# Two thirds of a feed-forward layer's first product by Winograd's seven block products instead of eight

## The chip, the cores and the metric

The kernel runs on one core of one Trainium2 chip. The metric is device time of one execution, in microseconds; a lower time is better. Times of unprofiled runs are given as a median. A profiled execution has its own time, and its span runs from its first to its last instruction. The engines are PE (matrix products; PEld is its loading of weights), DVE (vector), ACT (scalar functions), POOL, and SP, which issues the transfers.

## What is computed

A block-local attention feeds a two-layer feed-forward. Cut to what matters:

```python
# q, k, v: (8, 8, 576, 64); chunks of 64 positions, no attention across chunks
scores = scale * np.matmul(q_c, k_c.transpose(0, 1, 2, 4, 3))
attn = np.exp(scores - max); attn = attn / (sum + 1e-09)
x = np.matmul(attn, v_c)              # put together to (4608 tokens, 512)
h = x @ w_in                          # w_in  (512, 2048)
g = h - np.tanh(h)
out = (g @ w_out).astype(np.float32)  # w_out (2048, 512)
```

The two products of the feed-forward are nearly all of the arithmetic. Each float32 operand is kept as a high and a low part, and a product is three passes: high by high, low by high and high by low.

## The kernel before

The 4608 tokens are nine groups of 512. A group has four tiles of 128 tokens; the program also calls a tile a pair, since it holds two chunks of attention. For one group, `gemm1` makes 128 of the 2048 hidden columns (one `fc` of 16) for all 512 tokens: 3 passes by 4 slices `kc` of the contraction, 12 products with a moving operand of 512 columns, in one PSUM bank `ph`. `shrink` reads that bank: ACT makes the tanh, DVE subtracts, ACT and DVE make the two parts of `g` (`gh`, `gl`). `gemm2` takes the 128 hidden columns of `g` as weights, 12 products of 512 columns, into the four banks `po`. `FeedForward.run` lets `gemm2` follow `gemm1` by two `fc`s, so PE always has two `fc`s of `g` in hand.

Groups 0 and 1 have their parts in the type float32r. From group 2 on (`self.half`, L401) both layers use float16 parts. The weights are turned into float16 by `Half.convert`, three vector and scalar instructions for each `fc`: the 16 of the first layer and 3 of the second in group 1, the other 13 of the second layer in group 2. A converted tile is written over the float32 tile of the `fc` before.

The attention of group g+1 is worked while PE does the feed-forward of group g. The class `Late` has its steps, and `interleaved` puts them at half-steps of `run`: for each tile `split` (the values in two parts), `scores` (L157), `softmax` (L293 to L301), `transpose` (L307, L308 and a transposing transfer, L310) and `values` (L321), whose result goes into the parts `xh`, `xl` of the next group (L324, L325). `BASE` and `STEPS` say at which half-step; `values` is set ten half-steps after `split` and eight after `scores`. The order on each engine is set by a planner from priorities and its own costs. Only the beginning of the program has an order written out by hand (`PLAN`).

On each engine the instructions run in the order of the program. DVE and ACT carry both the `shrink` of the running group and the attention of the next; an instruction that waits holds up all behind it on that engine. SP issues loads, transposing transfers and stores in one order as well.

Of the kernel before, what the change touches and what calls it, by code (L numbers as in the profile page):

```python
# [11 lines left out]
F32 = mybir.dt.float32  # L12
F32R = mybir.dt.float32r
# [9 lines left out]
P = 128  # L23
# [16 lines left out]
WS = 2  # L40
AHEAD = 3
EARLY_FC = 8
# [15 lines left out]
def attn_ffn_kernel(ctx: ExitStack, tc: tile.TileContext, qkE, vE, qL, kL, vL, w_in, w_out, out):  # L58
# [38 lines left out]

    def new_half_x():

        t = xpool.tile([P, KC, MOST], F32R, name="xh").bitcast(F16)  # L100
        return t[:, :, :MOST], t[:, :, MOST:]

    def power(pool, name, sums, to, back):
# [10 lines left out]
        nc.vector.reciprocal(out=to, in_=back)  # L114

    def largest(a, out):

        nc.vector.tensor_reduce(out=out, in_=a, axis=AX.X, op=ALU.max, apply_absolute_value=True)
        nc.vector.tensor_scalar_mul(out, out, 2.0 ** -12)

# [119 lines left out]
    class Late:  # L240
# [4 lines left out]
        def __init__(self, pool):  # L245
            self.pool, self.st = pool, defaultdict(dict)

            self.raw = {n: xpool.tile([P, KC, MOST], F32R, name="xl").bitcast(F32) if n == "q" else pool.tile([P, MOST // P, H * CH], F32, name=f"raw{n}", bufs=1) for n in "qkv"}
            self.v16, self.a, self.aT = [], [], []
            self.room([pool.tile([P, 2, DM], F16, name=f"v16{a}", bufs=1).rearrange("p a n -> p (a n)") for a in "hl"])  # L250

        def two_banks(self):

            return ps_a.tile([P, 2, 4 * P], F32, name="psa")

# [5 lines left out]

        def load(self, p, i):
            for n, src in (("q", qL), ("k", kL), ("v", vL)):
                nc.sync.dma_start(out=self.raw[n][:, i], in_=src[p - NE])

        def powers(self, g):

            d = self.st[f"g{g}"]
            top, to, back = (self.pool.tile([P, 1], F32, name=n, bufs=2) for n in ("sums", "to", "from"))
            largest(self.raw["v"][:, :SIZES[g]].rearrange("p i n -> p (i n)"), top)  # L270
            power(self.pool, "x", top, to, back)
            d["to"] = to_x[g] = to
            from_x[g] = back

        def split(self, g, p, i):
            to = self.st[f"g{g}"]["to"]
            v = self.raw["v"][:, i].rearrange("p (a d) -> p a d", d=D)
# [6 lines left out]
        def scores(self, p, i):  # L284
            q, k = (self.raw[n][:, i].rearrange("p (hp c t) -> p hp c t", hp=4, c=2) for n in "qk")
            self.st[p]["ps"] = quarters(self.two_banks(), lambda r, hp, c: q[r, hp, c, :], lambda r, hp, c: k[r, hp, c, :], "u")

# [24 lines left out]

        def values(self, p, x, i):
            d = self.st.pop(p)
            xh, xl = x
            ps = self.two_banks()[:, 0].rearrange("p (hp c k) -> p hp c k", hp=4, c=2)
            for hp in range(4):
                for c in range(2):
                    cs = slice(c * CH, (c + 1) * CH)
                    for k, (a, b) in enumerate(((0, 0), (0, 1), (1, 0))):  # L320
                        nc.tensor.matmul(ps[:, hp, c, :], lhsT=self.v16[p % len(self.v16)][a][:, c, hp, :], rhs=d["a16"][:, b, hp, cs], start=(k == 0), stop=(k == 2))  # L321
            ts = slice(i * P, (i + 1) * P)
            ps = ps.rearrange("p hp c k -> p hp (c k)")
            nc.scalar.mul(xh[:, :, ts], ps, 2.0 ** -14)  # L324
            nc.vector.scalar_tensor_tensor(out=xl[:, :, ts], in0=ps, scalar=2.0 ** -14, in1=xh[:, :, ts], op0=ALU.mult, op1=ALU.subtract)  # L325

    def interleaved(att, g, x):

        at = defaultdict(list)
        base, first = (LATER, 5) if g == 2 else (BASE, 0)  # L330
        if g == 2:
            for i in range(SIZES[g]):
                at[0].append(lambda i=i: att.load(FIRST[g] + i, i))
        at[first + 2].append(lambda: att.powers(g))
        for i in range(SIZES[g]):
            p = FIRST[g] + i
            fs = [lambda p=p, i=i: att.split(g, p, i), lambda p=p, i=i: att.scores(p, i), lambda p=p: att.softmax(p),
                  lambda p=p: att.transpose(p), lambda p=p, i=i: att.values(p, x, i)]
            for k, f in zip(STEPS, fs):
                at[base[i] + k].append(f)  # L340
            if g + 1 < NG and i < SIZES[g + 1]:
                at[base[i] + STEPS[1] + 1].append(lambda i=i: att.load(FIRST[g + 1] + i, i))
        return at

    class Half:
# [4 lines left out]
        def __init__(self, pool):  # L350
            self.pool = pool
            self.to_h = const.tile([P, 1], F32, name="to_h")
            self.to, self.back = (const.tile([P, 2], F32, name=n) for n in ("to_w", "from_w"))

        def powers(self):
# [19 lines left out]
        def convert(self, part, fc, place):  # L375
# [6 lines left out]
            nc.vector.scalar_tensor_tensor(out=l16, in0=l, scalar=to, in1=l16, op0=ALU.mult, op1=ALU.add)  # L382

        def power_of(self, g):
            sig, to, undo = (const.tile([P, 1], F32, name=n, bufs=2) for n in ("sig", "to_g", "undo_g"))
            nc.vector.tensor_mul(sig, from_x[g], self.back[:, 0:1])
            nc.vector.scalar_tensor_tensor(out=to, in0=to_x[g], scalar=4.0, in1=self.to_h, op0=ALU.mult, op1=ALU.mult)
            nc.vector.tensor_scalar(out=to, in0=to, scalar1=2.0 ** 100, scalar2=TINY, op0=ALU.min, op1=ALU.max)
            nc.vector.reciprocal(out=undo, in_=to)
            nc.vector.tensor_mul(undo, undo, self.back[:, 1:2])  # L390
            return sig, to, undo


    class FeedForward:
# [3 lines left out]
        def __init__(self, g, x):  # L398
            self.g, self.x, self.queue, self.po = g, x, [], []
# [8 lines left out]
        def room(self, pool, tiles):  # L408
            self.po += [pool.tile([P, DM], F32, name=f"po{t}") for t in tiles]

# [53 lines left out]

        def finish(self):
            assert not self.queue
            for t in range(SIZES[self.g]):
                ot = outs[t] if outs else ffn.tile([P, DM], F32, name="t", bufs=3)
# [9 lines left out]
                r = (FIRST[self.g] + t) * P  # L478
                nc.sync.dma_start(out=out[r:r + P, :], in_=ot)


# [83 lines left out]
    att, half = Late(late), Half(late)  # L565
    for g in range(1, NG):
        x, nx = nx, new_half_x() if g + 1 < NG else None
        ff = FeedForward(g, x)
        ff.room(ps_o1, range(2))
        ff.room(ps_o2, range(2, SIZES[g]))  # L570
        at = interleaved(att, g + 1, nx) if nx else {}
        if g == 1:
            half.powers()
            first_place = late.tile([P, DM], F32, name="first_place", bufs=1).bitcast(F16)
            for fc in range(FC):

                at[2 * fc + 1].append(lambda fc=fc: half.convert(0, fc, place_of("l", 0, fc - 1) if fc else first_place))

            def more(k):

                t = [place_of("h", 0, fc) for fc in (range(6) if k == 0 else range(6, 12))]
                if k == 0:
                    att.room(t[0:2])
                    att.a += [a.rearrange("p (a n) -> p a n", a=2) for a in t[2:4]]
                else:
                    att.aT += [a.rearrange("p (i q) -> p i q", i=8) for a in t[0:2]]
                    outs.extend(a.bitcast(F32) for a in t[2:6])

            at[12].append(lambda: more(0))
            at[2 * FC + 2].append(lambda: more(1))  # L590

        for fc in range(FC):
            if g == (1 if fc < AHEAD else 2):
                k = 2 * FC + 2 * (LAG - AHEAD + fc) - 3 if g == 1 else 2 * (fc - AHEAD) + 1
                at[k].append(lambda fc=fc: half.convert(1, fc, place_of("l", 1, fc - 1) if fc else place_of("h", 0, 13)))
        ff.run([(fc, 0, SIZES[g]) for fc in range(FC)], at)

# [40 lines left out]
```

## Time and profile before

| | us |
|---|---|
| median of 3 runs (849.85 to 850.09) | 849.96 |
| the profiled execution | 849.57 |
| its span | 847.8 |
| PE busy | 829.4 (98%) |
| DVE busy | 536.2 (63%) |
| ACT busy | 396.7 (47%) |
| granted TensorE clock, mean | 0.992 |

The page has the share of the span that each engine was busy. A busy share is a mean over stages with different limits, so the stages are looked at apart: group 1 runs from about 140 to 228.5 us, group 2 from 228.5 to 316.8, and from there on every group takes 89 us. [...] Idle time of an engine that is not the bound costs nothing.

### The profile page before, as it was taken

The numbers are of one execution on the slowest core, as the hardware profiler recorded it, in microseconds if no ns is written. First come the engines' busy times: TensorE is split into PE (matmuls) and PEld (weight loads), VectorE is DVE, ScalarE is ACT, GpSimd is POOL, SyncE is SP. The second block draws the span as 40 slices with busy tenths as digits, with TensorE's granted clock in tenths as the row PEclk, the third lists the DMA queues.
The fourth block names the chain that finished last, engine by engine and source line by source line (L and its number), as shares of the span: only waits on it lengthen the run. The fifth ranks groups of instructions, "written<-read, shape, count | busy, mean of one in ns | idle before, by whom it ended". The sixth has DMA issues, their size and how long they took to land.

```text
span 847.8 us, 13865 instructions
## 1 busy us (share of the span) xinstructions
PE 829.4 (98%) x5645; PEld 458.1 (54%) x5645; DVE 536.2 (63%) x922; ACT 396.7 (47%) x729; POOL 8.7 (1%) x19
## 2 busy tenths in 40 slices
PE   5899999999999999999999999999999999999997
PEld 2687788778744444444444444444444444444443
DVE  5997897878997755565556555564567446633232
ACT  5898874445664443334343443434344334423222
POOL 0000001000000000000000000000000000000000
PEclk7899999999999999999999999999999999999999
DMA  9735234222212212221221121321222100110001
GB/s 358 278 110 200 100 101 149 63 52 74 75 51 68 58 44 81 51 74 27 88 63 50 51 86 39 76 50 63 63 55 59 50 14 13 20 56 1 1 1 50
DMA packets 53823, 62.76 MB, mean 74 GB/s; under 512 B 32256, under 2 KB 32256, under 8 KB 53760
## 3 DMA queue, kind: packets, MB, share of 16 engines
q1 hardware_dynamic: 53760, 61.88, 23.6%
q8 instruction: 44, 0.72, 0.3%
q14 instruction: 19, 0.16, 0.1%
HBM read 45.09 MB, written 9.44 MB: 64 GB/s over the span
## 4 chain that ended last, share of the span: by engine, by line
PE 87%; DVE 7%; ACT 3%; issue 1%; DMA 1%; SPq 0%; DVEq 0%; ACTq 0%
PE po L447 41%; PE ph L418 40%; PE psa L321 2%; PE psa L157 2%; DVE w L137 1%; DVE w L136 1%; DVE wl L382 1%; DVE wl L381 1%; ACT w L134 1%; ACT s L201 1%; ACT wh L141 1%; DMA raw<-w_out 1%; DVE wl L142 1%; DVE w L135 0%; PE ps L157 0%
## 5 line engine op out<-in xcount | busy, mean ns | idle before, releaser
L418 PE MATMUL ph<-xh,wl 128*128 128x512 f16 (+2 forms) x1404 | 324.3, 378 | 0.1
L447 PE MATMUL po<-wl,gh 128*128 128x512 f16 (+1 forms) x968 | 300.4, 381 | 0.0
L418 PEld LDWEIGHTS <-wl 128*128 128x128 f16 x1260 | 120.1, 98 | 140.7 <-issue 0.4
L447 PE MATMUL po<-wl,gl 128*128 128x512 f16 x420 | 159.2, 379 | 0.0
L434 DVE SCALAR_TENSOR_TENSOR gl<-t,to_g,gh 128x512 f16<-128x512 f32 x112 | 84.1, 751 | 108.4 <-ACT gh L433 108.4
L427 DVE SCALAR_TENSOR_TENSOR t<-ph,sig,t 128x512 f32<-128x512 f32 x112 | 83.8, 748 | 98.4 <-ACT t L426 97.8
L447 PEld LDWEIGHTS <-gh 128*128 128x128 f16 x896 | 87.3, 98 | 104.3
L433 ACT ACTIVATE gh<-t,to_g 128x512 f16<-128x512 f32 x112 | 80.8, 721 | 130.9 <-PE po L447 104.7
L426 ACT ACTIVATE t<-ph,sig 128x512 f32<-128x512 f32 x112 | 76.8, 685 | 117.6 <-PE ph L418 116.7
L447 PEld LDWEIGHTS <-gl 128*128 128x128 f16 x448 | 43.8, 98 | 52.8
L447 PE MATMUL po<-wh,gh 128*128 128x512 f32 (+1 forms) x184 | 67.7, 393 | 1.6 <-ACT gh L438 1.6
L447 PE MATMUL po<-wh,gl 128*128 128x512 f32 (+1 forms) x156 | 61.0, 393 | 0.2 <-DVE gl L439 0.2
L295 ACT ACTIVATE s<-s 128x512 f32<-128x512 f32 x28 | 17.6, 630 | 59.6 <-DVE s L294 59.4
L418 PE MATMUL ph<-xh,wh 128*128 128x512 f32 (+1 forms) x144 | 37.5, 377 | 1.7 <-ACT xh L237 1.2
L307 ACT CAST wh<-s 128x512 f16<-128x512 f32 x27 | 16.7, 618 | 45.9 <-DVE s L301 45.8
L418 PE MATMUL ph<-xl,wh 128*128 128x512 f32 (+1 forms) x144 | 35.6, 368 | 0.0
L380 ACT ACTIVATE wl<-wh,to_w 128x512 f16<-128x512 f32 x30 | 21.6, 722 | 24.0 <-DVE wl L382 12.7
L297 DVE TENSOR_REDUCE sm<-s 128x8 f32<-128x512 f32 x28 | 19.2, 685 | 18.2 <-ACT s L295 18.2
L418 PEld LDWEIGHTS ph<-xh,wh 128*128 128x128 f32 x144 | 24.9, 188 | 7.7 <-ACT wh L141 1.7
L308 DVE TENSOR_TENSOR wh<-s,wh 128x512 f16<-128x512 f32 x27 | 18.7, 692 | 15.9 <-ACT wh L307 15.7
L438 ACT CAST gh<-t 128x512 fp32r<-128x512 f32 (+1 forms) x36 | 20.5, 570 | 16.6 <-PE po L447 14.3
L447 PEld LDWEIGHTS po<-wh,gh 128*128 128x128 f32 x128 | 24.0, 188 | 7.5 <-ACT gh L438 2.5
(114 smaller groups left out, 840.8 us busy)
## 6 DMA issues: line engine op xcount, KB each, us to landing
raw<-w_in SPq DMA_DIRECT2D x16, 512.0 KB, 4.0
raw<-w_out SPq DMA_DIRECT2D x16, 512.0 KB, 5.0
out<-wh SPq DMA_DIRECT2D x32, 256.0 KB, 2.4
rawk<-kL SPq DMA_DIRECT2D x28, 256.0 KB, 3.0
rawv<-vL SPq DMA_DIRECT2D x28, 256.0 KB, 2.6
xl<-qL SPq DMA_DIRECT2D x28, 256.0 KB, 2.8
qk<-qkE SPq DMA_DIRECT2D x8, 512.0 KB, 5.7
v<-vE SPq DMA_DIRECT2D x8, 256.0 KB, 5.6
```

The source lines that it names most:

```text
L157: nc.tensor.matmul(ps[os, r, hp * CH:(hp + 1) * CH], lhsT=lhsT(rs, hp, o), rhs=rhs(rs, hp, o), start=True, stop=True)
L295: nc.scalar.activation(s, s, AF.Exp, scale=scale)
L297: nc.vector.reduce_sum(out=sm[:, :, 0], in_=s, axis=AX.X)
L308: nc.vector.tensor_sub(a[:, 1], sf, a[:, 0])
L380: nc.scalar.activation(h16, h, AF.Copy, scale=to)
L418: nc.tensor.matmul(ph, lhsT=self.weight(fc, 0, a)[:, kc * P:(kc + 1) * P], rhs=x[b][:, kc, cols], start=(k == 0), stop=(k == 3 * KC - 1))
L426: nc.scalar.activation(t, ph, AF.Tanh, scale=self.sig)
L427: nc.vector.scalar_tensor_tensor(out=t, in0=ph, scalar=self.sig, in1=t, op0=ALU.mult, op1=ALU.subtract)
L433: nc.scalar.activation(gh, t, AF.Copy, scale=self.to_g)
L434: nc.vector.scalar_tensor_tensor(out=gl, in0=t, scalar=self.to_g, in1=gh, op0=ALU.mult, op1=ALU.subtract)
L438: nc.scalar.copy(out=gh, in_=t)
L447: nc.tensor.matmul(self.po[t], lhsT=gg[a][:, ts], rhs=self.weight(fc, 1, b), start=(fc == 0 and i == 0), stop=(fc == FC - 1 and i == 2))
```

## The change

Groups 0 to 2 keep the first layer in eight block products; group 2 now does it in float32r. From group 3 on (`WINO = 3`) it is done by units of four `fc`s. A unit's weights are seen as two by two blocks A (two `fc`s by two halves of the contraction, for two such pairs of `fc`s, `q`), the tokens as two by two blocks B (two halves of the contraction by even and odd tiles). The four blocks of the result need seven products of sums of blocks instead of eight (Winograd's form). Each is 12 products of 256 columns: 2 `q`, 2 `kc`, 3 passes.

- The sums of weight blocks (`whole`, `sums`, `slots`) are made and cut into float16 parts in group 2. The second layer's 16 conversions all lie in group 1.
- The sums of token blocks (`Late.block`) are made as each tile's attention comes out, and stored as seven slots in two parts.
- Three PSUM banks X, Y and Z gather the products. X and Y are the two `ph` banks; Z is the first of the two banks that attention's scores use. A block of the result is a sum of two banks: ACT copies one of them into SBUF, DVE adds the other, and tanh and the rest of `shrink` go on from there. Z's first content is kept in `m5`.
- `chunk` is the second layer for one block: 12 products of 512 columns, three blocks behind at the least.
- From group 3 on PE's order is written out by hand in `unit`: Z, Y, chunk, X, Z, values, chunk, X, Y, chunk, scores, X, chunk. `scores` is for the tile that the next unit's `values` needs.
- Loads of q and k come two tiles ahead, those of v four tiles ahead, and the largest value is taken by tile (`Late.largest`).

```diff
-AHEAD = 3
+WINO = 3
+UNITS = 4
@@ class Late
+        def block(self, p, bank, x):
+            first, second, t12, t34 = self.blocks
+            cs = slice(p % 4 // 2 * P, (p % 4 // 2 + 1) * P)
+            def parts(slot, a):
+                h, l = (t[:, slot:slot + a.shape[1], :, cs] for t in x)
+                nc.scalar.copy(out=h, in_=a)
+                nc.vector.tensor_sub(l, a, h)
+            if p % 2 == 0:
+                nc.scalar.mul(first.rearrange("p s k n -> p (s k n)"), bank, 2.0 ** -14)
+                parts(0, first)
+                return
+            nc.scalar.mul(second.rearrange("p s k n -> p (s k n)"), bank, 2.0 ** -14)
+            nc.vector.tensor_sub(t12[:, 0], second[:, 0], first[:, 0])
+            nc.vector.tensor_sub(t12[:, 1], second[:, 1], t12[:, 0])
+            parts(3, t12)
+            nc.vector.tensor_sub(t34[:, 0], second[:, 1], second[:, 0])
+            nc.vector.tensor_sub(t34[:, 1], t12[:, 1], first[:, 1])
+            parts(2, second[:, 1:2])
+            parts(5, t34)
@@ class FeedForward
-            self.half = g > 1, g > 1
+            self.half = g >= WINO, g > 1
+    class Winograd:
+        def product(self, name, u, a, b, first=False):
+            bank = self.banks[name]
+            for q in range(2):
+                k = 0
+                for kc in range(2):
+                    for i, j in ((0, 0), (1, 0), (0, 1)):
+                        nc.tensor.matmul(bank[:, q * 2 * P:(q + 1) * 2 * P], lhsT=sums_w16[u][a][:, i, q, kc * P:(kc + 1) * P], rhs=self.x[j][:, b, kc, :], ...)
+        def shrink(self, u, i, half_, op, a, b):
+            ...
+            if b is not self.m5:
+                nc.scalar.copy(out=c, in_=b)
+                b = c
+            nc.vector.tensor_tensor(out=c, in0=a, in1=b, op=op)
+            nc.scalar.activation(t, c, AF.Tanh, scale=ff.sig)
+            nc.vector.scalar_tensor_tensor(out=c, in0=c, scalar=ff.sig, in1=t, op0=ALU.mult, op1=ALU.subtract)
+            nc.scalar.activation(gh, c, AF.Copy, scale=ff.to_g)
+            nc.vector.scalar_tensor_tensor(out=gl, in0=c, scalar=ff.to_g, in1=gh, op0=ALU.mult, op1=ALU.subtract)
+        def unit(self, ff, u, x, extra):
+            extra("start")
+            self.product("Z", u, 3, 3, True)
+            nc.scalar.copy(out=m5, in_=Z)
+            self.product("Y", u, 1, 1, True)
+            self.chunk()
+            self.product("X", u, 0, 0, True)
+            self.shrink(u, 0, 0, ALU.add, X, Y)
+            self.product("Z", u, 6, 2)
+            extra("values")
+            self.chunk()
+            self.product("X", u, 4, 4)
+            self.shrink(u, 0, 1, ALU.add, X, Z)
+            extra("middle")
+            self.product("Y", u, 2, 6, True)
+            self.chunk()
+            extra("scores")
+            self.product("X", u, 5, 5)
+            self.shrink(u, 1, 0, ALU.subtract, X, Y)
+            self.shrink(u, 1, 1, ALU.add, X, m5)
+            self.chunk()
+            extra("end")
```

Where instructions stand. DVE from the largest score of a tile to the instruction after which the transposing transfer can go (`mx` the largest, `s` the exponents, `sm` their sum, the last row the low part); before, while group 4 is in the feed-forward:

```order
L293 TENSOR_REDUCE mx<-psa 128x8
L294 TENSOR_TENSOR s<-psa,mx 128x512
L297 TENSOR_REDUCE sm<-s 128x8
L298 TENSOR_SCALAR sm<-sm 128x8
L299 RECIPROCAL sm<-sm 128x8
L300 TENSOR_SCALAR sm<-sm 128x8
L427 SCALAR_TENSOR_TENSOR t<-ph,sig,t 128x512
L301 TENSOR_TENSOR s<-s,sm 128x512
L308 TENSOR_TENSOR wh_1888<-s,wh_1888 128x512
```

The same piece of DVE now, in the third unit of group 4 (L590, L593 and L596 belong to `shrink`):

```order
L306 TENSOR_REDUCE mx<-psa 128x8
L307 TENSOR_TENSOR s<-psa,mx 128x512
L590 TENSOR_TENSOR wh_3554<-ph,wh_3554 128x512
L590 TENSOR_TENSOR spare<-ph,m_5027 128x512
L310 TENSOR_REDUCE sm<-s 128x8
L593 SCALAR_TENSOR_TENSOR wh_3554<-wh_3554,sig,t 128x512
L311 TENSOR_SCALAR sm<-sm 128x8
L593 SCALAR_TENSOR_TENSOR spare<-spare,sig,t 128x512
L312 RECIPROCAL sm<-sm 128x8
L596 SCALAR_TENSOR_TENSOR gh<-wh_3554,to_g,gh 128x512
L313 TENSOR_SCALAR sm<-sm 128x8
L596 SCALAR_TENSOR_TENSOR gl<-spare,to_g,gl 128x512
L314 TENSOR_TENSOR s<-s,sm 128x512
L321 TENSOR_TENSOR wh_1891<-s,wh_1891 128x512
```

Where one instruction of `shrink` stood inside the piece, six stand now.

DVE at the end of group 2 (L354, the token sums of the last tile of group 3; L554, an output of group 2 read out of `po`; L590, the first block of group 3):

```order
L354 TENSOR_TENSOR xl<-wh_2531,xh 128x4x128
L306 TENSOR_REDUCE mx<-psa 128x8
L554 TENSOR_SCALAR t<-po_2523,undo_g 128x512
L307 TENSOR_TENSOR s<-psa,mx 128x512
L273 TENSOR_REDUCE tops<-rawv 128x1
L310 TENSOR_REDUCE sm<-s 128x8
L311 TENSOR_SCALAR sm<-sm 128x8
L312 RECIPROCAL sm<-sm 128x8
L554 TENSOR_SCALAR t<-po_2525,undo_g 128x512
L313 TENSOR_SCALAR sm<-sm 128x8
```

The softmax of the first tile of group 4 stands behind the token sums of group 3, and the output of group 2 stands inside it.

More of the change, by code (lines that the diff above doesn't have):

```diff
@@ L327, in interleaved @@
     def interleaved(att, g, x):
         at = defaultdict(list)
-        base, first = (LATER, 5) if g == 2 else (BASE, 0)
+        base, first = (LATER, 7) if g == 2 else (BASE, 2)
+        ps = [FIRST[g] + i for i in range(SIZES[g])]
         if g == 2:
[L332 to L338, printed above, removed]
+            at[0] += [lambda p=p: att.load(p) for p in ps[:2]] + [lambda p=p: att.load_values(p) for p in ps]
+            at[first] += [lambda p=p: att.largest(p) for p in ps]
@@ L339, in interleaved @@
+        at[first].append(lambda: att.powers(g))
+        for p, b in zip(ps, base):
+            fs = (lambda p=p: att.split(p)), (lambda p=p: att.scores(p)), (lambda p=p: att.softmax(p)), (lambda p=p: att.transpose(p)), (lambda p=p: att.values(p, x))
             for k, f in zip(STEPS, fs):
-                at[base[i] + k].append(f)
-            if g + 1 < NG and i < SIZES[g + 1]:
-                at[base[i] + STEPS[1] + 1].append(lambda i=i: att.load(FIRST[g + 1] + i, i))
+                at[b + k].append(f)
+            at[b + 1].append(lambda p=p: att.load_values(p + 4))
+            at[b + 4].append(lambda p=p: att.largest(p + 4))
+            at[b + STEPS[1] + 1].append(lambda p=p: att.load(p + 2))
@@ L353, in __init__ @@
             self.to, self.back = (const.tile([P, 2], F32, name=n) for n in ("to_w", "from_w"))
+            self.w, self.s = {}, [{} for _ in range(UNITS)]
         def powers(self):
@@ L408, in room @@
         def room(self, pool, tiles):
-            self.po += [pool.tile([P, DM], F32, name=f"po{t}") for t in tiles]
+            self.po.update((t, pool.tile([P, DM], F32, name=f"po{t}")) for t in tiles)
         def gemm1(self, fc, t0, t1):
@@ L565, in attn_ffn_kernel @@
     att, half = Late(late), Half(late)
-    for g in range(1, NG):
-        x, nx = nx, new_half_x() if g + 1 < NG else None
+    sums_w16 = [{} for _ in range(UNITS)]
+    spare = late.tile([P, DM], F32, name="spare", bufs=1)
+    places = {}
+    for g in (1, 2):
+        x, nx = nx, new_x() if g + 1 < WINO else new_sums_of_x()
         ff = FeedForward(g, x)
@@ L575, in attn_ffn_kernel @@
             for fc in range(FC):
[L577 to L595, printed above, removed]
-        ff.run([(fc, 0, SIZES[g]) for fc in range(FC)], at)
+                at[2 * (fc + LAG) + 1].append(lambda fc=fc: half.convert(1, fc, place_of("l", 1, fc - 1) if fc else first_place))
@@ new lines, in attn_ffn_kernel, with extra @@
+        ff.run([(fc, 0, SIZES[g]) for fc in range(FC)], at)
+    att.banks = ps_a.tile([P, 2, 4 * P], F32, name="psa")
+    w = Winograd(dict(X=ps_h.tile([P, MOST], F32, name="ph"), Y=ps_h.tile([P, MOST], F32, name="ph"), Z=att.banks[:, 0]))
+    w.cs += [spare] + [place_of(*places[u][7], F32) for u in (2, 3)]
+    rest = half.sums(UNITS - 1) + half.slots(UNITS - 1, places[UNITS - 1])
+    with tc.manual_schedule(engines={E.PE}):
+        for g in range(WINO, NG):
+            x, nx = nx, new_sums_of_x() if g + 1 < NG else None
+            ff = FeedForward(g, x)
+            for u in range(UNITS):
+                p = FIRST[g + 1] + u if nx else NPAIR
+                def extra(where):
+                    if where == "start" and p < NPAIR:
+                        att.split(p)
+                        att.load_values(p + 4)
+                    elif where == "values":
+                        if p < NPAIR:
+                            att.values(p, nx)
+                    elif where == "middle" and p < NPAIR:
+                        att.largest(p + 4)
+                    elif where == "scores" and p + 1 < NPAIR:
+                        att.scores(p + 1)
+                        att.softmax(p + 1)
+                        att.transpose(p + 1)
+                        att.load(p + 3)
+                    elif where == "end" and u == UNITS - 1 and p + 1 < NPAIR:
+                        att.powers(g + 2)
+                    if g == WINO and u < UNITS - 1:
+                        for _ in range(1):
+                            if rest:
+                                rest.pop(0)()
+                w.unit(ff, u, x, extra)
+                if g == WINO and u == UNITS - 1:
+                    assert not rest, len(rest)
+                    outs += [place_of(*places[UNITS][k], F32) for k in range(4)]
+        while w.chunks:
+            w.chunk(0)
```

166 lines of the change are left out of this document (132 added, 34 removed).

## The prediction

> **What bounds the kernel now.** First the page's chain of the work that ended last, then the windows table (group 1, group 2, group 3), then the timeline of PE.
>
> ```profile
> PE 87%; DVE 7%; ACT 3%; issue 1%; DMA 1%; SPq 0%; DVEq 0%; ACTq 0%
> ```
> ```profile
> core 0: us, PE busy (x) PEld busy (x) DVE busy (x) ACT busy (x) POOL busy (x), PEclk, DMA share, GB/s
> 140.00:228.50 88.50, 88.50 (x581) 70.91 (x581) 76.07 (x137) 45.57 (x73) 1.27 (x3) 1.00 0.20 51
> 228.50:316.80 88.30, 88.18 (x607) 42.03 (x607) 66.50 (x110) 42.96 (x66) 0.35 (x1) 1.00 0.22 61
> 316.80:405.80 89.00, 89.00 (x612) 42.40 (x611) 51.80 (x89) 36.04 (x55) 0.35 (x1) 1.00 0.22 61
> ```
>
> From group 1 on PE never stops and the clock is 1.00: these stages are PE's bound. DVE has 37 us free in group 3 and 22 in group 2. What a product costs is the distance between starts:
>
> ```profile
> 301.11 2.75 PE L418 MATMUL ph<-xh,wl 128*128 128x512 f16 x12
> ...
> 306.29 2.75 PE L418 MATMUL ph<-xh,wl 128*128 128x512 f16 x12
> ```
> ```profile
> 311.47 0.86 PE L321 MATMUL psa<-wh,wh 128*128 128x64 f16 x24
> 312.17 0.60 PE L447 MATMUL po<-wl,gh 128*128 128x512 f16 x2
> ```
> ```profile
> 122.35 1.07 PE L418 MATMUL ph<-xh,wh 128*128 128x512 f32 x4
> ...
> 125.07 1.07 PE L418 MATMUL ph<-xh,wh 128*128 128x512 f32 x4
> ```
>
> Between the first two starts lie 12 of gemm1 and 12 of gemm2: 5.18/24 = 215.8 ns for 512 columns. The values' 24 products of 64 columns take 0.70 us, 29.2 ns each. The line through both is 0.4165 ns a column plus 2.5 ns, so 256 columns cost 109.2 ns. In float32r 512 columns cost 2.72/12 = 226.7 ns.
>
> **Part 1, seven products for eight (-28.4).** Group 3 and later: 192 products of 215.8 ns (41.43 us) become 4 units x 7 x 12 = 336 of 109.2 ns (36.69 us): 4.74 us less a group, 28.4 in six. gemm2 and attention keep their counts. The rate of 256 columns is bounded by early float32r rows of that width: four starts in 0.48 us, 120 ns. At 120 the part would be worth only 6 x (41.43 - 40.32) = 6.7 us; but float32r carries 11 ns at 512 columns too (226.7 against 215.8), so I keep 109.2.
>
> ```profile
> 52.02 0.64 PE L418 MATMUL ph<-xh,wl 128*128 128x256 f32 x4
> 52.50 0.64 PE L418 MATMUL ph<-xl,wh 128*128 128x256 f32 x4
> ```
>
> Weight loads, now one per 109 ns, are printed at 98 ns, and the values' stream shows them spaced 29 ns apart under products, so they stay hidden.
>
> ```profile
> L321 PEld LDWEIGHTS <-v16l 128*128 128x128 f16 x112 | 9.9, 98 | 0.0
> ```
>
> [...]
>
> **Part 2, group 2 in float32r (+2.1).** 192 x (226.7 - 215.8) ns = 2.1 us.
>
> **Part 3, the hand-over from group 2 to 3 (+6, 3.5 to 11).** Group 2 loses 9 or 10 conversions on DVE (two of 0.75 us each, -14) and gains 14 `whole` (0.68), 32 `sums` of 256 columns (0.41), 22 splits of 256 (0.45, estimated between the two rows below) and 16 of 512 (0.75), 5.2 us of token sums (8.1 by these rows for 2.9 now) and 3.4 of a fifth softmax: 9.5+13.1+9.9+12+5.2+3.4 = 53.1 on.
>
> ```profile
> L427 DVE SCALAR_TENSOR_TENSOR t<-ph,sig,t 128x512 f32<-128x512 f32 x112 | 83.8, 748 | 98.4 <-ACT t L426 97.8
> L430 DVE TENSOR_TENSOR t<-ph,t 128x512 f32<-128x512 f32 x28 | 19.1, 682 | 1.2 <-ACT t L429 1.2
> L430 DVE TENSOR_TENSOR t<-ph,t 128x256 f32<-128x256 f32 x8 | 3.3, 410 | 0.3 <-ACT t L429 0.3
> ```
>
> 66.5 - 14 + 53.1 = 106 us of printed durations. Neighbours that don't need each other overlap by 0.08 us (starts at 245.10 and 245.76 for 0.74), which makes it 92 at best; with waits for ACT as in today's full stretch it is near 100.
>
> ```profile
> 245.10 0.74 DVE L427 SCALAR_TENSOR_TENSOR t<-ph,sig,t 128x512 f32<-128x512 f32 x1
> 245.76 0.16 DVE L298 TENSOR_SCALAR sm<-sm 128x8 f32<-128x8 f32 x1
> ```
>
> PE needs 88.3 + 2.1 + 0.7 (the fifth scores) = 91 for group 2. DVE is level with PE or late by up to 9. Of that some 5 us pass unseen (two `fc`s of g in hand). Then comes what cannot be hidden: the scores of group 4's first tile stand before the last gemm2; its values follow after 2.6 + 4 x 1.31 = 7.8 us of PE, while the softmax, with two outputs of group 2 inside it, takes some 8 us (6.1 by the rows of part 4, the outputs 0.75 each, and the wait for the first) and the transposing transfer 3.1 (below). 8 + 3.1 - 7.8 = 3.3 with DVE on time, up to 11 with DVE late; I take 6.
>
> **Part 4, values waiting for scores (+12.7, 0 to 28).** Today the pair of these rows has 22 us between its scores and its values:
>
> ```profile
> 344.08 0.69 PE L157 MATMUL psa<-rawk,xl 64*64 64x64 f32 x32
> ...
> 366.87 0.86 PE L321 MATMUL psa<-wh,wh 128*128 128x64 f16 x24
> ```
>
> In `unit` there are five products and two chunks between: 60 x 0.1092 + 24 x 0.2158 = 11.73 us. What must fit, from the timeline of one pair:
>
> ```profile
> 433.31 2.76 PE L418 MATMUL ph<-xh,wl 128*128 128x512 f16 x12
> 433.33 0.75 DVE L434 SCALAR_TENSOR_TENSOR gl<-t,to_g,gh 128x512 f16<-128x512 f32 x1 [1.66 <-ACT gh L433]
> 433.44 0.34 SPq L264 DMA_DIRECT2D xl<-qL  x1
> 433.83 1.87 SPq L264 DMA_DIRECT2D rawk<-kL  x1
> 434.00 0.68 DVE L293 TENSOR_REDUCE mx<-psa 128x8 f32<-128x512 f32 x1
> 434.71 0.69 DVE L294 TENSOR_TENSOR s<-psa,mx 128x512 f32<-128x512 f32 x1
> 435.44 0.63 ACT L295 ACTIVATE s<-s 128x512 f32<-128x512 f32 x1 [2.14 <-DVE s L294]
> 436.10 0.69 DVE L297 TENSOR_REDUCE sm<-s 128x8 f32<-128x512 f32 x1 [0.70 <-ACT s L295]
> ...
> 437.35 0.74 DVE L427 SCALAR_TENSOR_TENSOR t<-ph,sig,t 128x512 f32<-128x512 f32 x1
> 438.01 0.68 DVE L301 TENSOR_TENSOR s<-s,sm 128x512 f32<-128x512 f32 x1
> ...
> 440.09 1.25 SPq L310 DMA_TRANSPOSE wh<-wh  x1
> ```
> ```profile
> rawv<-vL SPq DMA_DIRECT2D x28, 256.0 KB, 2.6
> ...
> wh<-wh SPq DMA_TRANSPOSE x24, 3.1
> ```
>
> From the largest's start to the transfer's issue: 6.09 us, one foreign instruction (L427) inside. Now six stand there. If the holes (0.7 us for the exponent, the small steps) took all five more, it stays 6.1; if none, 6.09 + 5 x 0.75 = 9.8. Setting them down one by one, each behind its own tanh or `gh` of 0.7 us on ACT, I get 8.2. So L = M + 8.2 + 3.1 + 0.05 = M + 11.35, where M is how late after the scores DVE comes to the largest. The wait of PE is M - 0.4 us, and nothing is left over: values hold up all PE work behind them, since PE's order is fixed.
>
> M for the four units of a group: 1.5 where two outputs (L554, 0.75 each) stand just before; 1.0 to 1.7 in the two odd units, whose token sums (seven instructions and two splits after values) push the block X+Z back, and where `largest` waits for its load of 2.6 us issued only after the second split; 0.2 in the other. A wait in one unit lets the next start with DVE less behind. That gives 1.4 + 1.1 + 0.7 + 0.1 = 3.3 a group: groups 4 to 6, 9.9; group 7, with no loads or largest left, 1.9; group 3, whose first unit is in part 3, 0.9. Sum 12.7 for 19 waits, 0.67 each. If L were 0.8 shorter nothing would remain; if 0.8 longer, some 28.
>
> **Edits at no cost.** DVE's work for a later group is 120 instructions, 70.8 us by these rows' durations, against 84 of PE; ACT's, counted the same way, some 50. PE comes back to a PSUM bank 3.9 us after leaving it at the least, so copies and additions hide under products (uncovered, 0.6 us each). On SP the loads of q and k (433.44 to 435.70 above) are long out when the transposing transfer comes, and they stand ahead of it today as well. Group 1 has 16 conversions where it had 19. The end keeps three chunks (7.8 us) over the last chain of 4 us.
>
> **Sum.** -28.4 + 2.1 + 6 + 12.7 = -7.6 on the profiled 849.57: 842.0. The runs' median lies 0.4 above that execution: 842.4.
>
> **Rivals.**
> A, the chain fits: the holes swallow the additional instructions, L under 11.7. Only part 3 at its low end stays: 849.96 - 28.4 + 2.1 + 3.5 = 827. For it: DVE is only three quarters full. Against: in-order engines, six instructions with their own waits inside.
> B, the other side: each values wait costs over 1.07 us, the point where 19 of them eat 28.4 - 2.1 - 6 = 20.3. Place: the transposing transfer behind the softmax on DVE. At 1.5 us (L 0.8 longer: M and the six instructions both near their upper bound) it is 28.5, and the time 858. For it: the equality of L and the window, and that `largest` waits for a load on DVE just ahead of the chain. Against: a late unit gives the next one slack.
> C, exposed weight loads, as a mechanism of this kernel: 144 more a group x 98 ns x 6 = 84.7 us, some 927 with the rest. Speaks against it: the 29 ns.
>
> **Numbers.** Forecast (834 to 848.2) 0.52, A 0.17, C 0.02, B 0.20, and 0.09 for the strip between. A measurement of this kernel can tell 0.2%, 1.7 us, from no change: faster 0.69, same 0.09, slower 0.22. The forecast's own range is 834 to 848; with A's low end (827) and B (858) less their outer parts, 826 to 856.
>
> **What would show it.** PE starts of 256-column products 109 ns apart (120 or more breaks part 1); group 2 in about 97 us with PE idle at its end behind DVE (no idle: part 3 falls); in each later group some 3 us of PE idle ahead of values, released by the transposing transfer, mostly in the first and odd units (none: A; over 4.3 a group: B); later groups near 87.5 us, the last near 80. Waits of PE on banks X, Y or Z would make the prediction wrong in a way not listed.

## The result, and the profile after

The changed kernel takes 845.74 us (median; 844.87 to 846.38) against 849.94 us: a ratio of 0.995, 95% interval 0.993 to 0.997. It is faster by 0.5%, where 0.9% (842.4 us) was forecast; the range held the time. The profiled execution took 846.38 us with a span of 844.6 us, 3.2 us less than that of before.

The time by stages of the changed kernel, from the table of windows (busy time of each engine, then the granted clock). The windows are the second part of group 2, the hand-over to group 3 up to its first chunk, and two later groups from chunk to chunk.

```profile
core 0: us, PE busy (x) PEld busy (x) DVE busy (x) ACT busy (x) POOL busy (x), PEclk, DMA share, GB/s
...
262.00:326.00 64.00, 59.99 (x437) 37.01 (x436) 62.91 (x134) 40.94 (x72) 0.72 (x1) 1.00 0.20 51
326.00:342.40 16.40, 14.03 (x140) 10.99 (x141) 10.43 (x20) 8.60 (x14) 0.00 (x0) 0.79 0.33 102
342.40:429.40 87.00, 84.39 (x756) 56.38 (x754) 64.92 (x120) 47.86 (x78) 0.37 (x1) 1.00 0.21 59
429.40:516.40 87.00, 84.31 (x754) 56.31 (x752) 64.81 (x121) 47.70 (x78) 0.37 (x1) 1.00 0.22 62
```

Three things are to be seen. In group 2 VectorE is busy 62.9 of 64 us, and TensorE is not full. In the hand-over the granted clock is 0.79. In the later groups TensorE is idle some 2.6 us of 87 while VectorE has 22 us to spare, so there it is an order of work, not a load, that costs the time.

What TensorE waited for, from the table of waits (total, times, longest), and then the two idle times of the hand-over and the rows behind them, from the timeline (start, duration, operation, idle time before it and its releaser):

```profile
PE psa L334 <- DMA wh<-wh: 12.1, 13, 2.4
...
PE psa L577 <- DVE s L307: 3.1, 1, 3.1
```
```profile
326.02 0.38 PE L577 MATMUL psa<-xh,wh 128*128 128x256 f16 x2 [3.09 <-DVE s L307]
...
326.97 0.63 PE L577 MATMUL psa<-xh,wh 128*128 128x256 f16 x2
...
329.97 0.38 PE L577 MATMUL ph<-xh,wh 128*128 128x256 f16 x2
...
335.43 0.22 PE L334 MATMUL psa<-wh,v16h 128*128 128x64 f16 x2 [2.35 <-DMA wh<-wh]
...
336.96 0.64 PE L577 MATMUL ph<-xh,wh 128*128 128x256 f16 x2
...
340.51 0.69 PE L153 MATMUL psa<-rawk,rawq 64*64 64x64 f32 x32
```

Thirteen value products waited for the transposing transfer, one block product, the first into Z, for VectorE's softmax row L307, which reads the scores out of the same `psa`. The forecast had the waits for the landing and a VectorE that is late at the end of group 2; it had no wait of a product into Z, and it did not have the rows of 0.63 for two products: behind each of the two idle times the products of 256 columns follow one another at some 213 ns instead of 109, for about 3.4 us (the granted clock is 0.66 in 325 to 330 us and again in 335 to 340), and then at the full rate again (0.38 for two).

The steady rate of these products, from the timeline of group 4: 24 of them lie between the first row and the last.

```profile
431.98 0.38 PE L577 MATMUL psa<-xh,wl 128*128 128x256 f16 x2
...
434.60 1.46 PE L613 MATMUL po<-first_place,gl 128*128 128x512 f16 x6
```

2.62 us / 24 = 109.2 ns, as forecast. And the chain of one unit of group 4, from the timeline of three engines: the largest on VectorE, the issue of the transposing transfer on SP's queue, the values on TensorE.

```profile
429.28 0.68 DVE L306 TENSOR_REDUCE mx<-psa 128x8 f32<-128x512 f32 x1
...
437.48 1.24 SPq L323 DMA_TRANSPOSE wh<-wh  x1
...
440.56 0.63 PE L334 MATMUL psa<-wh,wh 128*128 128x64 f16 x16 [0.59 <-DMA wh<-wh]
```

8.20 us to the issue and 3.08 to the landing, where 8.2 and 3.1 were forecast (6.09 to the issue before the change).

An idle row costs 0.165 us more than it prints, an estimate from two figures of this trace: a product of 256 columns is printed at 0.27 us (273 ns in the mean), and where nothing holds the next, it starts 0.109 after it. With this the 3.2 us come apart as follows. The idle rows of the hand-over (0.94 ahead of the last scores, 3.09 and 2.35) make 6.9 us with what is added to them; the slow products behind them take 3.4 us more than at 109.2 ns; the 12 other waits of values, 12.1 - 2.35 = 9.8 us, make 11.7; float32r in group 2 costs some 3.3. This is an account of TensorE's time in the profiled execution: what each item would give back if it alone were gone is for the experiments to tell. What is left over for the seven products is 28.8 us: from group 3's first product (317.35 before, 326.02 after) to the end the span is 530.45 us before and 518.58 after, 11.9 less, although 2.35 + 0.17 + 3.4 + 11.7 us of losses lie in it; 0.7 of that gain is the scores that moved into group 2.

### The profile page after: what moved, and what is told of

The parts are those of the page before. It is cut to its first block, busy times and chain, and to the rows that moved or that the text cites. A ratio compares the mean times of both kernels' runs of the same rounds, so it can differ in the third digit from the quotient of the medians.

```text
span 844.6 us, 15882 instructions
## 1 busy us (share of the span) xinstructions
PE 809.8 (96%) x6507; PEld 560.4 (66%) x6509; DVE 633.9 (75%) x1175; ACT 478.6 (57%) x897; POOL 8.9 (1%) x19
## 4 chain that ended last, share of the span: by engine, by line
PE 60%; DVE 22%; ACT 9%; DMA 7%; issue 2%; SPq 0%; DVEq 0%; POOL 0%; ACTq 0%; POOLq 0%
PE po L613 20%; PE ph L577 13%; PE ph L501 10%; PE po L530 10%; PE psa L577 4%; DMA wh<-wh 4%; DMA rawv<-vL 2%; PE psa L334 2%; DVE wh L590 1%; DMA raw<-w_out 1%; DVE wh L593 1%; PE psa L153 1%; ACT xh L353 1%; ACT wh L293 1%; DVE xl L354 1%
## 5 line engine op out<-in xcount | busy, mean ns | idle before, releaser
L613 PE MATMUL po<-wl,gh 128*128 128x512 f16 x540 | 124.4, 379 | 0.0
L577 PEld LDWEIGHTS <-wh 128*128 128x128 f16 x1080 | 105.6, 99 | 26.4 <-issue 3.6
L577 PEld LDWEIGHTS <-wl 128*128 128x128 f16 x936 | 91.5, 98 | 18.3
L577 PE MATMUL ph<-xh,wh 128*128 128x256 f16 x528 | 92.2, 277 | 0.0
L530 PE MATMUL po<-wl,gh 128*128 128x512 f32 (+1 forms) x248 | 86.3, 388 | 0.0
L577 PE MATMUL ph<-xh,wl 128*128 128x256 f16 x432 | 73.7, 273 | 0.0
L577 PE MATMUL ph<-xl,wh 128*128 128x256 f16 x264 | 73.0, 277 | 0.0
L590 DVE TENSOR_TENSOR wh<-ph,wh 128x512 f32<-128x512 f32 x48 | 33.0, 688 | 42.5 <-PE ph L577 41.5
L593 DVE SCALAR_TENSOR_TENSOR wh<-wh,sig,t 128x512 f32<-128x512 f32 x64 | 47.6, 748 | 18.3 <-ACT t L592 17.9
L577 PE MATMUL ph<-xl,wl 128*128 128x256 f16 x216 | 58.9, 273 | 0.0
L501 PE MATMUL ph<-xh,wl 128*128 128x512 f32 (+1 forms) x208 | 53.4, 377 | 0.0
L530 PE MATMUL po<-wh,gh 128*128 128x512 f32 x128 | 51.0, 399 | 1.6 <-ACT gh L521 1.6
L530 PE MATMUL po<-wh,gl 128*128 128x512 f32 x128 | 50.5, 397 | 0.2 <-DVE gl L522 0.2
```

Source lines behind the costliest of these rows:

```text
L501: nc.tensor.matmul(ph, lhsT=self.weight(fc, 0, a)[:, kc * P:(kc + 1) * P], rhs=x[b][:, kc, cols], start=(k == 0), stop=(k == 3 * KC - 1))
L530: nc.tensor.matmul(self.po[t], lhsT=gg[a][:, ts], rhs=self.weight(fc, 1, b), start=(fc == 0 and i == 0), stop=(fc == FC - 1 and i == 2))
L577: nc.tensor.matmul(bank[:, q * 2 * P:(q + 1) * 2 * P], lhsT=sums_w16[u][a][:, i, q, kc * P:(kc + 1) * P], rhs=self.x[j][:, b, kc, :], star ...
L590: nc.vector.tensor_tensor(out=c, in0=a, in1=b, op=op)
L593: nc.vector.scalar_tensor_tensor(out=c, in0=c, scalar=ff.sig, in1=t, op0=ALU.mult, op1=ALU.subtract)
L613: nc.tensor.matmul(ff.po[t], lhsT=g[a][:, ts], rhs=half_w[1][fc][:, b], start=(first and s == 0 and k == 0), stop=(last and s == 1 and k = ...
```

## The experiments

Seven kernels were run. All but the two with additional products make the same computation as the changed kernel, in another order or on another engine. Each diff is against the changed kernel unless it says otherwise. Medians are compared with its 845.74 us; the ratios are to the kernel before, timed beside each.

### The values one chunk later

```diff
             self.product("Z", u, 6, 2)
-            extra("values")
             self.chunk()
+            extra("values")
             self.product("X", u, 4, 4)
```

> Each value product group of attention is issued one chunk of weight preparation later inside its unit, so that the window between the maximum's start and the first value product grows from 11.7 to about 14.3 us, against the 11.6 to 13.1 us that the chain (issue after 8.2, landing 3.1, the maximum's own lateness 0.1 to 1.4) takes in the changed kernel's trace. Theory (the wait on the landing is what the seven-product groups lose, about 11.7 us with the drains, of which the hand-over's 2.35 us is one): all of these waits are gone, the time is 845.7 - 11 to 13 = 832 to 835 us, the later groups 84.5 to 85.5 us each. Rival (the wait only moves: the values' sums come out of their bank later, and the next unit's scores or the second block of products wait for that bank, or VectorE is late instead): 843 us or more, with new idle time of TensorE of the same size behind a row of VectorE.

Measured: 834.35 us (834.17 to 835.85), ratio 0.982 (0.981 to 0.983), 11.4 us less than the changed kernel. Its table of waits:

```profile
PE psa L577 <- DVE s L307: 3.1, 1, 3.1
PE psa L334 <- DMA wh<-wh: 2.5, 2, 2.3
```

(A chunk is the second layer's 12 products for one block; the expectation calls it weight preparation.) The waits for the landing went from 13 to 2, and nothing took their place; from chunk to chunk a later group takes 83.8 to 84.2 us, a little less than expected. The one that stayed is the 2.35 us of the hand-over: in the first unit of group 3 there is no chunk to put in front of the values yet, which the expectation had overlooked. So the waits of the values were the loss of the later groups: 9.6 us of waits less, with 0.165 for each of the 11, make the 11.4.

### The values one block product earlier

```diff
             self.shrink(u, 0, 0, ALU.add, X, Y)
-            self.product("Z", u, 6, 2)
             extra("values")
+            self.product("Z", u, 6, 2)
             self.chunk()
```

> The value products are issued one block product earlier, 12 products of 109.2 ns = 1.31 us, so the window is 10.4 us instead of 11.7. Theory (window against chain): every unit that waits now waits 1.31 us more (13 of them), and of the six units that just do not wait now each waits by about 1.0 us; +17 to +23 us: 862 to 869 us. Rival (the waits shown are not what holds the path, VectorE is as late elsewhere): within 4 us of 845.7.

Measured: 883.49 us (881.84 to 884.62), ratio 1.039 (1.038 to 1.041): 38 us slower, and well outside both expectations. Its table of waits, and the rows of one unit and of another from its timeline:

```profile
PE psa L334 <- DMA wh<-wh: 27.7, 20, 3.7
PE psa L577 <- ACT wh L357: 7.4, 10, 1.3
PE psa L577 <- ACT wh L360: 6.9, 10, 0.7
```
```profile
450.03 0.87 PE L334 MATMUL psa<-wh,wh 128*128 128x64 f16 x24 [1.93 <-DMA wh<-wh]
451.59 0.38 PE L577 MATMUL psa<-xh,wh 128*128 128x256 f16 x2 [0.69 <-ACT wh L360]
...
452.87 0.63 PE L577 MATMUL psa<-xh,wh 128*128 128x256 f16 x2
...
545.29 0.87 PE L334 MATMUL psa<-wh,wh 128*128 128x64 f16 x24 [1.95 <-DMA wh<-wh]
546.85 0.38 PE L577 MATMUL psa<-xh,wh 128*128 128x256 f16 x2 [0.69 <-ACT wh L360]
```

The waits for the landing grew by 15.6 us over 20 units, somewhat less than the theory's 17 to 23. The rest was not expected. Bank Z and the bank of the values are the two halves of one tile, `psa`, and the product into Z that now comes right behind the values waits each time until ScalarE has read the values (L357, L360): 20 times, 14.4 us. The 27 additional idle rows add 27 x 0.165 = 4.5, and in three places products run at half rate that did not in the changed kernel, some 4 us: at 452 us, at 640, and in the first group, where the stretch behind the landing lasts 6.8 us (336.4 to 343.2) for 3.4; the mean clock of the profiled execution is 0.982, and 0.988 in the changed kernel. These make 38.5 us. In the changed kernel a chunk lies between the values and the next product into `psa`, and covers this read. No run gave the two banks tiles of their own.

### The first softmax of group 4 six half-steps earlier in group 2

```diff
             at[31].append(lambda: att.powers(WINO + 1))
-            at[34] += [lambda: att.scores(p), lambda: att.softmax(p), lambda: att.transpose(p), lambda: att.load(p + 2)]
+            at[28] += [lambda: att.scores(p), lambda: att.softmax(p), lambda: att.transpose(p), lambda: att.load(p + 2)]
```

> The scores, the softmax and the transposing load of group 4's first tile, which stand at half-step 34 of group 2 (behind its last hidden chunks), are put at half-step 28. Theory (the hand-over's 6.4 us idle comes from that softmax's rows at the end of VectorE's queue, ahead of the activation rows and the weight sums, and from the landing behind it; the half clock of the products behind each idle time costs 3.5 us more): the idle times of 0.94, 3.09 and 2.35 us shrink to less than 2 us together, the granted clock of the hand-over goes from 0.79 to 0.95 or more, and the time is 845.7 - 7 to 10 = 836 to 839 us. Rival 1 (VectorE's whole load in group 2 is the cause: 62.9 of 64 us busy): the same idle time shows up earlier in group 2, and the time stays at 844 to 847 us.

Measured: 841.24 us (840.81 to 842.88), ratio 0.990 (0.989 to 0.992): 4.5 us less than the changed kernel, less than the theory's 7 to 10 and more than the rival's none. The scores of the second unit stand at 333.33 instead of 340.51, from its timeline, and the values behind them now wait longer:

```profile
333.33 0.69 PE L153 MATMUL psa<-rawk,rawq 64*64 64x64 f32 x32
...
348.42 0.86 PE L334 MATMUL psa<-wh,wh 128*128 128x64 f16 x24 [1.70 <-DMA wh<-wh]
```

So the hand-over itself gained 7.2 us, as the theory said, with a granted clock of 1.00 all through it; the next unit gave 2.6 back, 1.9 of it to this wait and 0.8 to a product into Z that waits 0.62 us for VectorE's row L307 (at 338.74). VectorE's load did not vanish either: ahead of that, four idle times of TensorE in the hand-over are left, 2.3 us in all, the longest 1.15 us ahead of `xl` from L354.

### Filling the idle times with products

Additional products go ahead of group 3's first block product and ahead of its first values; nothing else is changed.

```diff
+            def fill(bank, n):
+                w0 = half_w[1][0][:, 0]
+                for _ in range(n if ff.g == WINO and u == 0 else 0):
+                    nc.tensor.matmul(bank, lhsT=w0[:, :P], rhs=w0, start=True, stop=True, skip_group_check=True)
+            fill(X, 14)
             self.product("Z", u, 3, 3, True)
...
             self.product("Z", u, 6, 2)
+            fill(att.banks[:, 1], 11)
             extra("values")
```

> Additional work: 14 products of 512 columns ahead of group 3's first block product and 11 ahead of its first values, written into banks that the next real product overwrites; they keep TensorE busy (14 x 216 ns = 3.0 us, 11 x 216 = 2.4 us) while it waits today for VectorE and for the transposing landing. Nothing else changes. Theory (the products behind the two idle times run at half the clock, because the engine was idle, and lose 1.75 + 1.8 us): the products behind both run at 109 ns for 256 columns at once, the granted clock of the hand-over rises from 0.79 to about 1.00, the time is 845.7 - 3 to 4 = 842 us (841.5 to 843). Rival 1 (the half clock follows from something else, such as the load after it): clock 0.79 still, time 845.5 to 846.5 us. Rival 2 (the additional products come late and stand in the path): 847 to 850 us.

Measured: 845.83 us (845.21 to 847.88), ratio 0.996 (0.994 to 0.997): no difference to the changed kernel. But its hand-over is another, from the windows and the timeline:

```profile
326.00:342.40 16.40, 15.51 (x163) 11.42 (x161) 11.82 (x23) 8.79 (x15) 0.00 (x0) 1.00 0.40 127
```
```profile
330.77 0.38 PE L577 MATMUL psa<-xh,wl 128*128 128x256 f16 x2 [0.89 <-ACT m L629]
...
337.87 0.69 PE L153 MATMUL psa<-rawk,rawq 64*64 64x64 f32 x32
...
678.00 0.22 PE L334 MATMUL psa<-wh,v16h 128*128 128x64 f16 x2 [1.74 <-DMA wh<-wh]
```

The clock is 1.00 and the slow rows are gone, although the same products follow; so they come from the idle time and not from the load behind it. The second unit's scores come 2.6 us earlier (337.87 against 340.51) and not 3.4, since the faster products now run into a copy of ScalarE. In the profile 2.2 us of this last until the first values of group 7, where one landing came 4.5 us after its issue (at 673.46) and not 3.1. Whether that happened in the other executions can't be seen. So the clock was settled by this run and its price was not. The price need not be the same in every execution either: the four of the changed kernel have mean clocks, over the whole execution, of 0.986 to 0.993, and that with 0.993 took 845.26 us, 1.1 less than the profiled one with 0.988.

### The same with the values one chunk later

Both edits together, so that no landing can eat the gain.

```diff
+            fill(X, 14)
             self.product("Z", u, 3, 3, True)
...
             self.product("Z", u, 6, 2)
-            extra("values")
             self.chunk()
+            fill(att.banks[:, 1], 11)
+            extra("values")
```

> The values one chunk later (834.35 us alone, with the hand-over still at a granted clock of 0.66 in 325 to 330 us and in 335 to 340 us) together with the 25 additional products of 512 columns that fill TensorE's two idle times there and are overwritten. In the run of the fill alone the hand-over was 2.6 us shorter in the profile, but the median did not move, and one landing that took 4.5 us instead of 3.1 ate 1.4 us of it. Here no values wait for a landing after the hand-over, so nothing can eat it. Theory (half the clock behind an idle time is a cost of its own, about 2.6 us of path): clock 1.00 in the hand-over, 831 to 832.5 us. Rival (what lies behind at half the clock is covered by VectorE's chain, so the clock costs nothing): clock 1.00 and 833.5 to 835 us.

Measured: 832.01 us (831.00 to 832.94), ratio 0.979 (0.977 to 0.980), where the later values alone had 0.982 (0.981 to 0.983). The windows of the hand-over, of the later values alone and then with the fill:

```profile
325.00:345.00 20.00, 16.81 (x157) 12.60 (x158) 13.77 (x26) 10.05 (x16) 0.00 (x0) 0.83 0.38 125
```
```profile
325.00:345.00 20.00, 19.30 (x193) 14.25 (x191) 15.69 (x30) 11.20 (x19) 0.00 (x0) 1.00 0.39 125
```

2.3 us less between the medians (the slowest execution with the fill, 832.94, is faster than the fastest without, 834.17), and 2.2 between the two profiles from the second unit of group 3 on. The 25 additional products, 5.4 us of TensorE's time, made the kernel faster. So the half rate has a price of its own here, some 2.3 us of the 3.4 that the products lose.

### Later values and the earlier softmax

The first and the third edit together, a version that might beat both kernels.

> Both edits that gained alone: the value products one chunk later, and the first softmax of group 4 at half-step 28 of group 2. Alone, the early softmax was 7.2 us ahead at the second unit of group 3 and gave back 2.6 us at that unit's values, which then waited 1.70 us for the landing. Theory (that give-back is the same wait for the landing, and the window with a chunk more in it covers it): 834.4 - 7.2 + 0.5 = 827.6 us, 826.5 to 829, with no wait for the landing of more than 0.3 us and a granted clock of 1.00 in the hand-over. Rival (the give-back comes from VectorE, which is loaded in the hand-over as before): 829.5 to 831.5 us, the wait shown ahead of other products.

Measured: 828.26 us (827.99 to 828.42), ratio 0.974 (0.973 to 0.976): 2.6% faster than before, 17.5 us less than the changed kernel, and within the theory's 826.5 to 829. Its chain of waits by engine, which was 60% TensorE, 22% VectorE and 7% transfers in the changed kernel, and one full group:

```profile
PE 78%; DVE 14%; ACT 4%; DMA 2%; issue 1%; SPq 0%; DVEq 0%; POOL 0%; ACTq 0%; POOLq 0%
```
```profile
425.85:509.70 83.85, 83.85 (x754) 56.37 (x753) 64.57 (x121) 47.76 (x79) 0.37 (x1) 1.00 0.23 64
```

TensorE has no hole in it. From group 3's first product to the end it is 503.14 us, 27.3 less than before; with 2.1 us of waits still in it and the 0.7 of moved scores, the seven products are worth 28.7 us here too. So 1.9 of the 2.6 us that the third experiment gave back were the wait for the landing, which is gone. The rest was VectorE's, as the rival said, and stays: the product into Z still waits 0.63 us for L307 (at 338.28), about what the time lies above the theory's 827.6.

### The sums of the weights on GpSimd

Against the kernel of the run before:

```diff
             t = place_of("h", 0, fc - 1, F32) if fc else spare
-            nc.vector.tensor_add(t, h, l)
+            nc.gpsimd.tensor_add(t, h, l)
             self.w[fc] = t.rearrange("p (j n) -> p j n", j=2)
```

> As the run before, and the 16 sums of the high and low weights (128x512, float32) go from VectorE to GpSimd, so that VectorE has 16 x 0.61 = 9.8 us less to do in group 2, where it is busy 62.9 of 64 us. Theory (the 2.95 us that TensorE still waits at the end of group 2 are VectorE's load): these waits fall to less than 1 us, 825 to 826.5 us. Rival (GpSimd, on which no trace here shows such an addition, is slower than VectorE and delivers the sums late, or holds the powers of the attention behind them): the same waits or longer, 827.5 to 835 us.

Measured: 832.74 us (832.62 to 834.12), ratio 0.980 (0.978 to 0.982): 4.5 us slower than with the sums on VectorE, by the rival. GpSimd's group and VectorE's costliest group in group 2, from the groups by form of this run; then the latter with the sums on VectorE; then rows of this run's timeline:

```profile
L431 POOL TENSOR_TENSOR wh<-wh,wl 128x512 f32<-128x512 f32 x15 | 20.6, 1374 | 72.5 <-PE ph L501 65.4 <-issue 6.9
```
```profile
L517 DVE SCALAR_TENSOR_TENSOR gl<-t,to_g,gh 128x512 f16<-128x512 f32 x16 | 14.4, 900 | 0.2
```
```profile
L517 DVE SCALAR_TENSOR_TENSOR gl<-t,to_g,gh 128x512 f16<-128x512 f32 x16 | 11.9, 745 | 1.0 <-ACT gh L516 1.0
```
```profile
278.15 1.37 POOL L431 TENSOR_TENSOR wh<-wh,wl 128x512 f32<-128x512 f32 x1 [4.56 <-PE ph L501]
...
279.02 0.69 DVE L307 TENSOR_TENSOR s<-psa,mx 128x512 f32<-128x512 f32 x1
...
289.24 2.36 DVE L354 TENSOR_TENSOR xl<-wh,xh 128x512 f16<-128x512 f32 x2
289.64 1.40 POOL L431 TENSOR_TENSOR wh<-wh,wl 128x512 f32<-128x512 f32 x1 [4.11 <-PE ph L501]
```

A sum takes 1.37 us on GpSimd and 0.685 on VectorE, and VectorE's own rows grow while one runs: L517 from 745 to 900 ns in the mean, and at 289 us two of L354 take 2.36 us for 1.28, with GpSimd at work from 289.64 to 291.04. L307, which reads the scores from PSUM, keeps its 0.69 at 279.02 us, though GpSimd is at work from 278.15 to 279.52. VectorE got none of its 9.8 us back: from 228.5 us to group 3's first product it is busy 93.5 us, where it was 91.1 with the sums on it. Of the rows named, the two that grew read two large tiles in SBUF each (L354 `wh` and `xh`, L517 `t` and `gh`), and L307, which did not, takes its large one from PSUM. By what way the sums lengthen them, no run shows.

In the profiled execution, the slowest of the four, TensorE lost time in three places: 2.75 us of idle ahead of the values at 301 us, behind a softmax that came late; 3.9 us of waits at the end of group 2 for 2.35; and a stretch at half rate, with no idle time over 1.23 us near it. Two windows, the one ahead of the stretch and the stretch itself:

```profile
326.50:329.90 3.40, 1.60 (x12) 0.90 (x10) 3.34 (x8) 2.40 (x4) 0.00 (x0) 1.00 0.10 22
329.90:333.40 3.50, 3.50 (x20) 2.43 (x18) 2.44 (x6) 0.58 (x1) 0.00 (x0) 0.51 0.81 279
```

How much of the loss is the longer rows of VectorE and how much the sums that each come 0.7 us later, no run parts. And whether the last 3 us of waits at the end of group 2 are VectorE's load stays open: this run did not lighten it.

## Why the prediction was nearly right, point by point

**Part 1, seven products for eight (-28.4): right.** 109.2 ns a product, and 28.8 and 28.7 us are left for the part in the accounts of two kernels. Rival C, exposed weight loads, fell: L577 has 2016 loads of 128x128, 98 to 99 ns each in the mean, for its 2016 products, and these still start 109.2 ns apart where they run at the full rate.

**Part 2, float32r in group 2 (+2.1): mis-sized, some +3.3.** The step took 226.7 ns from one stretch of the profile before, at 122 us. In group 2 of the changed kernel, and then in the profile before at 133 us, from the timelines:

```profile
243.26 0.61 PE L530 MATMUL po<-wl,gh 128*128 128x512 f16 x2
...
248.66 0.61 PE L530 MATMUL po<-wl,gh 128*128 128x512 f16 x2
```
```profile
133.26 1.10 PE L418 MATMUL ph<-xh,wh 128*128 128x512 f32 x4
...
141.69 0.40 PE L447 MATMUL po<-wh,gh 128*128 128x512 f32 x1
```

5.40 us hold 12 products in float16 and 12 in float32r. With the float16 ones at 215.8 ns, 234 are left for each of the others; later in the group, 228 to 232. The profile before had that rate too: 36 products in float32r, with none in float16 among them, lie in the 8.43 us from 133.26 to 141.69, 234 ns each. So the neighbours in float16 are not the reason, and the step took the lower of two rates that its own profile shows. Why there are two wasn't tried.

**Part 3, the hand-over (+6, 3.5 to 11): right in its mechanism, mis-sized, 10.3.** The step's chain, from the timeline of the changed kernel: the scores on TensorE, the largest on VectorE, the issue of the transfer.

```profile
319.54 0.70 PE L153 MATMUL psa<-rawk,rawq 64*64 64x64 f32 x32 [0.94 <-ACT wh L360]
...
323.94 0.68 DVE L306 TENSOR_REDUCE mx<-psa 128x8 f32<-128x512 f32 x1
...
332.36 1.24 SPq L323 DMA_TRANSPOSE wh<-wh  x1
```

VectorE came to the largest 3.8 us after the scores (which ended at 320.17), the issue came 8.4 us later and the landing after 3.1 more, at 335.43: 15.3 us against the 7.8 of TensorE's work that the step had counted. So the values were 7.4 us late, where 6 had been taken out of 3.3 to 11, and VectorE was late as worked out. The wait of the product into Z for L307 and the first stretch at half rate lie within these 7.4 us. On top came two things that the step put at nothing: 1.1 us ahead of the scores, which waited until ScalarE had read the values before them out of `psa` (L360), and the 1.7 us of the second stretch at half rate, behind the landing. The first stretch also made the chain longer: in the middle of the softmax VectorE sat idle for 0.84 us ahead of L554 (at 328.54) until that slow product had ended. So of the 4.3 us that the step was low, some 2.5 are the clock, which it left out; the runs with additional products put it at 2.6 (the hand-over alone) and 2.3 (the medians).

**Part 4, the values' waits (+12.7): right.** 11.7 measured. The chain was 8.2 + 3.1 us as worked out, within 0.1 us in all four units of group 4. What differs between the units is how late VectorE comes to the largest: 1.9, 1.1, 1.3 and 0.1 us behind the scores, where 1.5, 1.0 to 1.7 and 0.2 had been estimated; less 0.4, as the step has it, this gives the waits. The waits were fewer and longer, 12 of 0.98 us for 19 of 0.67, and by units 1.3, 0.6, 0.75 and none for 1.4, 1.1, 0.7 and 0.1. The later values showed that this is all there is to it, since the time went down by what the waits had been. The sensitivity was not well sized. The step gives 15.8 us more waiting for 0.8 us of chain (28.5 for 12.7, and rival B 858 us); with 1.3 us less of window the waits grew by 15.6 us only. The time rose to 883 us all the same, because a wait of the next product for ScalarE and more half-rate stretches came with it. That is a mechanism which no rival had.

**Edits at no cost: right for this order of work only.** Behind the hand-over the changed kernel has no wait of TensorE on X, Y or Z. In the hand-over it has one: the 3.09 us of the first product into Z. The prediction said that such a wait would make it wrong in a way not listed. The wait was for the same softmax that held up the values behind it, so by the chain above it added nothing of its own. And the chunk behind the values covers 0.69 us a unit, as the earlier values showed, and the prediction's "3.9 us after leaving it" spoke of the banks without seeing that the values' bank and Z are one tile.

**Sum.** Against the profiled 846.38 the sum was 4.4 us low: +4.3 in part 3, +1.2 in part 2, -1.0 in part 4, -0.4 in part 1, 0.3 not traced. Group 2 took 97.4 us (228.59 to 326.02), where about 97 were forecast. Later groups, forecast near 87.5 us, were 86.1 to 87.0.

## What to carry to other kernels

Where an engine works in a fixed order, add up two things: its work between the instruction that starts a chain (here the scores) and the one that needs what the chain's transfer brings (the values), and the chain itself. When the two are equal, one more piece of work in front of the second instruction can be worth more than a change has won (11.4 us here for one moved line, against 4.2 for the whole change). An idle time on TensorE has to be priced with the slower products behind it where they follow (here 3.4 us lost behind 3.09 and 2.35 us of idle, some 2.3 of it in the time). Moving work off the full engine may take back what it gives (here 4.5 us slower, with L517 of VectorE grown from 745 to 900 ns while GpSimd had the sums).

## What the runs showed of the hardware that was not expected

- **Half rate behind some idle times and not behind others.** Products ran at 213 ns for 256 columns, for 3.4 us each time and once for 6.8, behind idle times of 3.09 and 2.35 us; in two places of the earlier values behind 1.93 + 0.69 and 1.85 + 0.69 us, with 24 value products between (at 452 and 640 us); and with the sums on GpSimd behind 0.65 + 1.15 us. At 545 us 1.95 + 0.69 left the rate at 109, and so did 0.37 + 1.15 at 323 us of the run with the later values and the earlier softmax. So length alone doesn't decide: the 1.8 us of the GpSimd run were followed by the half rate, and the 2.64 us at 545 us were not. What does decide, no run shows.
- **Additional products can shorten a kernel**, by 2.3 us for 25 of them, when they stand in idle time ahead of a dense stretch; in the other run that had them the median did not move.
- **float32r has no single rate here**: 512 columns took 227 ns at 122 us of the profile before and 234 at 133 us, both with float32r alone, and 228 to 234 between float16 products. The cause is open.
- **One landing of the transposing transfer took 4.5 us for 3.1**, in one execution, for no cause that the profile shows.
